# One pair of tiles in a streamed decode kernel: the last 8 KB of each row in loads of 112, 8 and 8 rows

## The chip, the cores and the metric

The kernel runs on one core of a Trainium2 chip. The metric is device time of one execution, in microseconds, median of several runs. The profile is one execution taken by the hardware profiler; its span goes from the first to the last instruction of the program.

## The reference

A decoder layer for one token of each of four sequences (B = 4, D = 512), with modulation from a conditioning vector, cached attention with grouped heads, and a token-mixing MLP:

```python
mod = (_silu(c) @ w_mod).reshape(c.shape[0], 6, 1, -1)
sa, ca, ga, sb, cb, gb = (mod[:, 0], ..., mod[:, 5])
h = _layernorm(x) * (1 + ca) + sa
x = x + ga * attention(h, k_cache, v_cache, wq, wo)
h = _layernorm(x) * (1 + cb) + sb
x = x + gb * mixer(h, w1, b1, w2, b2)
```

Attention has 32 query heads of 128 in groups of four on 8 key/value heads, and 4096 cached positions: q = h @ wq, softmax(q k^T / sqrt(128)) v, then @ wo. The mixer is a layer norm, an outer product with w1 (1792 wide), a gelu and a product with w2. All is float32. The caches are 4 x 8 x 4096 x 128 floats each, 67 MB for the keys and 67 MB for the values; with wq, wo and w_mod 157 MB are read.

## The kernel before

There are NS = 32 tiles, one for each sequence and key/value head. Tile i needs a key tile (128 rows of head dimension x 4096 positions, 16 KB a row) and a value tile (128 rows, each with 32 positions x 128, 16 KB a row). The host lays them out so that `kv[i]` holds the key tile of i + 2 beside the value tile of i: 128 rows of 32 KB, 4 MB, loaded by one transfer in `load_pair` (L176) into a buffer `kv` of shape [128, 2, 4096]. The buffers come from a ring of three (`slots`), shared with wq and parts of w_mod, so a load is issued on the sync engine's queue (SP) when all readers of the load three places before are done.

For each tile the kernel runs, in this order of names: `scores` (L231, 8 matmuls of the key tile against the queries into `s`), `row_max`, `turn_max`, `col_max`, `spread_max`, `copy_max`, `expo` (softmax over 1024 columns x 4 groups of rows, exponentials on the scalar engine), `turn` (a transpose on the vector engine), `sums` and `scale` (the denominators), `values` (L291, 8 matmuls of the value tile against the weights into `pv`; k = 0 to 3 read the first half of each value row, k = 4 to 7 the second half), `copy_v`, `pick`, `copy_o`, `project` (wo) and `add_up`. The mixer of a finished sequence runs in pieces between the tiles of the next.

The instructions of each engine stand in the order in which the program writes them; nothing is reordered. A loop over i = 0 to 23 issues the load of pair i + 1, works on the scores of tile i + 2, and on the values of tile i. Pair 16, issued in the pass i = 15, brings the key tile of 18, read by `scores(18)` in the pass i = 16, and the value tile of 16, read by `values(16, 0..3)` and `values(16, 4..7)` later in the same pass.

The last tiles follow an order written out by hand (a plan of steps). There the key and value tiles come in separate transfers: `load_key` (L197) for keys 30 and 31, `load_v` (L204) for values 28 to 31, the last one cut into five pieces, and `load_wm5` (L192) for the last part of w_mod. The output is written by L575 and L578.

Of the kernel before, what the change touches and what calls it, by code (L numbers as in the profile page):

```python
# [14 lines left out]
B, D, HQ, HKV, SK, DH, F = 4, 512, 32, 8, 4096, 128, 1792  # L15
# [7 lines left out]

WIDE = {NS - 5: 24, NS - 4: 32}
NARROW = NS - 3


@with_exitstack
def adaln_decode(ctx: ExitStack, tc: tile.TileContext, small, x, wmod, wq, kk, kv, vv, wo, out):
    nc = tc.nc  # L30
# [22 lines left out]
    for k in range(0, 4, 2):  # L53
        t = ring.tile([P, 2, HQ * DH], F32, name=f"wq{k}", tag="kv")
# [72 lines left out]
    for k in range(4):  # L127
        n = slice(k * P, (k + 1) * P)
# [20 lines left out]
    rows = cst.tile([B, B, 8], F32, name="rows")  # L149
# [9 lines left out]
    def slots():  # L159
        return ring.tile([P, 2, SK], F32, name="kv", tag="kv")  # L160

    def key(t, i):
        KT[i] = t

    def value(t, i):
        VT[i] = t.rearrange("p (j d) -> p j d", d=DH)
# [6 lines left out]

    def load_pair(i):
        t = slots()
        nc.sync.dma_start(t, kv[i])  # L176
        key(t[:, 0], i + 2)
        value(t[:, 1], i)

# [428 lines left out]

    load_first()
    load_pair(0)  # L610
    load_wo(0)
    for i in range(2):
# [4 lines left out]
    mix = None  # L617
    for i in range(NS - HKV):
        load_pair(i + 1)
        if i in (1, 3, 5):  # L620
            load_wo(i + 1)
# [62 lines left out]
    for step in PLAN.split():  # L684
        op, k = step.rstrip("0123456789."), step.lstrip("abcdefghijklmnopqrstuvwxyzABCDEFGHIJKLMNOPQRSTUVWXYZ")
        i, q = (int(n) for n in (k + ".0").split(".")[:2]) if k else (0, 0)
# [6 lines left out]
        elif op == "v":  # L693
            if i < NS - 2:
                (values if i < NARROW else values_narrow)(i, range(4 * q, 4 * q + 4))
                continue
# [92 lines left out]
```

## Time and profile before

| what | value |
|---|---|
| median of 3 runs | 386.49 us (386.43 to 388.0) |
| span of the profiled execution | 384.7 us (its own time outside the span isn't recorded) |
| TensorE matmul busy (PE) | 298.7 us, 78% |
| vector engine busy (DVE) | 198.2 us, 52% |
| scalar engine busy (ACT) | 112.2 us, 29% |
| bytes moved | 157.69 MB, 410 GB/s over the span |
| mean granted TensorE clock | 0.883 |

How to read it: the page has the busy time of each engine, the span in 40 slices, the transfer queues, the chain of work that ended last (followed back from the last instruction to what released each step), the costliest groups of instructions with the idle time before them, and the transfers with their issue. The trace behind it answers for one stretch of time, one tile or one engine. PE is the matmul engine, PEld its weight loads, SP the sync engine, which here only issues transfers. The transfers of the core run on 16 DMA engines; a share of 1.00 is all of them busy.

### The profile page before, as it was taken

To read this page: it belongs to the slowest core of one execution; us is meant where nothing else is said; L and a number is where in the kernel's file an instruction comes from. 1 tells how busy PE (TensorE), PEld (TensorE's weight loads), DVE (VectorE), ACT (ScalarE), POOL (GpSimd) and SP (SyncE) were. 2 spreads that over 40 slices of the span, in tenths; PEclk is the share of its full clock that TensorE was granted. 3 is DMA by queue.
4 is the path that set the end of the run, shared out by engine and by line. 5 is a ranking of instruction groups with operands and counts; after the bars stand their busy time and mean duration, and the time that the engine had idled before them with its cause. 6 is when DMAs were issued, how large, how long until landed. Compare 5 with 4: busy or idle time off the path is not lost.

```text
span 384.7 us, 5604 instructions
## 1 busy us (share of the span) xinstructions
PE 298.7 (78%) x2380; PEld 117.2 (30%) x2380; DVE 198.2 (52%) x407; ACT 112.2 (29%) x144; POOL 7.7 (2%) x33
## 2 busy tenths in 40 slices
PE   0856777866966949979877878788888887999984
PEld 0112122311323313334322222342222343333653
DVE  1130251620451424664866545557665567778757
ACT  1001111121110110212567311124575105657276
POOL 1100000000000000000000000000000000000000
PEclk9989555985695685998999998999999999999999
DMA  8999999999999999999999999999999999999930
GB/s 331 433 433 436 411 453 433 409 432 436 423 441 433 434 436 436 434 436 431 429 425 433 428 433 434 429 433 431 429 434 436 434 436 432 424 417 423 418 122 3
DMA packets 7409, 157.69 MB, mean 410 GB/s; under 512 B 964, under 2 KB 1236, under 8 KB 1496
## 3 DMA queue, kind: packets, MB, share of 16 engines
q1 hardware_dynamic: 7376, 157.33, 95.4%
q8 instruction: 18, 0.29, 0.3%
q14 instruction: 7, 0.06, 0.0%
q10 hardware_dynamic: 8, 0.00, 0.0%
HBM read 157.32 MB, written 0.01 MB: 409 GB/s over the span
## 4 chain that ended last, share of the span: by engine, by line
DMA 60%; PE 29%; DVE 7%; ACT 2%; issue 1%; POOL 0%; SPq 0%; POOLq 0%; DVEq 0%
DMA kv<-in_kv 58%; PE s L231 8%; PE pv L291 7%; PE s L122 2%; PE qs L138 2%; DVE m L236 2%; DVE p L267 2%; DMA sm<-in_small 2%; PE pa L343 2%; PE pt L328 2%; ACT uu L562 1%; PE pb L251 1%; PE pve L303 1%; PE pm L240 1%; PE pgx L348 1%
## 5 line engine op out<-in xcount | busy, mean ns | idle before, releaser
L231 PE MATMUL s<-kv,QT 128*32 128x512 f32 x512 | 75.2, 714 | 38.9 <-DMA kv<-in_kv 37.0
L236 DVE TENSOR_REDUCE m<-s 128x1 f32<-128x1024 f32 x32 | 39.2, 1224 | 96.0 <-PE s L231 95.9
L261 ACT ACTIVATE p<-s,nm 128x1024 f32<-128x1024 f32 x32 | 35.7, 1115 | 180.6 <-DVE nm L256 180.5
L291 PE MATMUL pv<-kv,p 128*32 128x512 f32 x464 | 69.8, 670 | 0.7 <-DMA kv<-in_kv 0.7
L231 PEld LDWEIGHTS s<-kv,QT 128*32 128x32 f32 x512 | 15.8, 123 | 84.0 <-DMA kv<-in_kv 52.5
L328 PEld LDWEIGHTS pt<-g,po 128*128 128x128 f32 x236 | 31.1, 205 | 27.2 <-issue 19.9
L343 PE MATMUL pa<-wo,oT 128*32 128x512 f32 x240 | 34.6, 648 | 4.6 <-DVE oT L335 4.4
L328 PE MATMUL pt<-g,po 128*128 128x4 f32 (+2 forms) x236 | 33.9, 267 | 1.5 <-DVE po L314 1.0
L267 DVE STREAM_TRANSPOSE p<-p 128x1024 f32<-128x1024 f32 x25 | 30.9, 1234 | 0.0
L314 DVE COPY po<-pv 128x512 f32<-128x512 f32 x29 | 20.0, 688 | 16.8 <-PE pv L291 16.7
L245 DVE TENSOR_REDUCE mx<-pm 1x128 f32<-1x512 f32 x32 | 21.3, 669 | 1.1 <-PE pm L240 1.1
L442 DVE TENSOR_SCALAR u<-hb,wr,sm 128x512 f32<-128x512 f32 x40 | 19.9, 541 | 1.9 <-POOL wr L437 1.0
L506 ACT ACTIVATE u<-u 128x1024 f32<-128x1024 f32 x20 | 20.4, 1051 | 1.5 <-DVE u L442 1.4
L361 DVE TENSOR_TENSOR acc<-acc,pa 128x512 f32<-128x512 f32 x26 | 17.8, 686 | 4.3 <-PE pa L343 4.2
L261 ACT ACT_TABLE_LOAD x11 | 14.1, 1283 | 20.3 <-DVE nm L256 20.2
L251 PEld LDWEIGHTS pb<-neg,mx 1*128 1x128 f32 x64 | 10.4, 202 | 28.2 <-DVE mx L245 26.5
L122 PE MATMUL s<-wm,sT 128*4 128x512 f32 x16 | 9.1, 732 | 10.6 <-DVE sT L108 10.6
L506 ACT ACT_TABLE_LOAD x13 | 16.7, 1283 | 0.2
L291 PEld LDWEIGHTS pv<-kv,p 128*32 128x32 f32 x464 | 13.4, 146 | 7.2 <-issue 3.1
L240 PE MATMUL pm<-ident,m 128*1 128x128 f32 x32 | 9.3, 289 | 7.4 <-DVE m L236 3.5
L251 PE MATMUL pb<-neg,mx 1*128 1x1 f32 x64 | 13.1, 271 | 2.1 <-DVE mx L245 2.1
L453 PE MATMUL py<-u,sm 128*32 128x512 f32 x80 | 14.4, 616 | 0.0
(158 smaller groups left out, 214.7 us busy)
## 6 DMA issues: line engine op xcount, KB each, us to landing
kv<-in_kv SPq DMA_DIRECT2D x28, 4096.0 KB, 21.9
wq<-in_wq SPq DMA_DIRECT2D x2, 4096.0 KB, 16.3
wo<-in_wo SPq DMA_DIRECT2D x4, 2048.0 KB
kv<-in_kv SPq DMA_DIRECT2D x4, 2048.0 KB, 20.3
wm<-in_wmod SPq DMA_DIRECT2D x2, 2048.0 KB, 14.8
kv<-in_kk SPq DMA_DIRECT2D x1, 4096.0 KB
kv<-in_vv SPq DMA_DIRECT2D x3, 1024.0 KB
wm<-in_wmod SPq DMA_DIRECT2D x1, 1024.0 KB
```

Source lines behind the costliest of these rows:

```text
L231: mm(s[32 * c:32 * c + 32, n * 512:(n + 1) * 512], QT[:, b, h, :], KT[i][:, (n * 4 + c) * 512:(n * 4 + c + 1) * 512], start=True, stop=True)
L236: dv.tensor_reduce(M[i], S[i], axis=AX.X, op=OP.max)
L245: dv.tensor_reduce(mx, M[i].rearrange("o (c r) -> o r c", c=4).unsqueeze(1).to_broadcast([1, 4, 32, 4]), axis=AX.X, op=OP.max)
L251: mm(pb, M[i].rearrange("o c r -> o (c r)"), neg1, start=True, stop=True)
L261: nc.scalar.activation(p, S[i], AF.Exp, bias=M.pop(i), accum_out=l)
L267: dv.transpose(PL[i][0], PL[i][0])
L291: mm(PV[i][32 * q:32 * q + 32, :], pT[:, 128 * k:128 * k + 128:4], VT[i][:, 4 * k:4 * k + 4, :].rearrange("p j d -> p (j d)"), start=(k < ...
L314: dv.tensor_copy(PV[i], pv)
L328: mm(pt, po[:, c * DH:(c + 1) * DH], sel.unsqueeze(1).to_broadcast([P, m, REP]), start=(c == 0), stop=(c == n - 1))
L343: mm(pa[32 * g:32 * g + 32, :], oT[:, g:g + 1].to_broadcast([P, 32]), wo_t[h][:, g, :], start=True, stop=True)
L442: dv.tensor_scalar(u[:, e, :], hb, wr[:, j:j + 1], b1[:, j:j + 1], op0=OP.mult, op1=OP.add)
L506: nc.scalar.activation(u, u, AF.Gelu_apprx_tanh)
```

## The change

The load of pair 16 is cut. The first 24 KB of each row (the key tile and the first half of the value tile) come in one transfer of 128 rows. The last 8 KB of each row (the second half of the value tile) come in three: rows 0 to 111, rows 112 to 119, rows 120 to 127. The same bytes go to the same places; all other loads stay as they are.

```diff
 WIDE = {NS - 5: 24, NS - 4: 32}
 NARROW = NS - 3
+UNEVEN = 16
...
     def load_pair(i):
         t = slots()
-        nc.sync.dma_start(t, kv[i])
+        if i == UNEVEN:
+            main = SK + SK // 2
+            rows, src = t.rearrange("p s n -> p (s n)"), kv[i].rearrange("p s n -> p (s n)")
+            nc.sync.dma_start(rows[:, :main], src[:, :main])
+            for lo, hi in ((0, 112), (112, 120), (120, 128)):
+                nc.sync.dma_start(rows[lo:hi, main:], src[lo:hi, main:])
+        else:
+            nc.sync.dma_start(t, kv[i])
         key(t[:, 0], i + 2)
         value(t[:, 1], i)
```

## The prediction

> **What bounds the kernel now.** I read the slices of the page first, then the chain that ended last, the stretches of time around the changed load and at the end of the stream, and then the matmul timeline at the places where the chain passes from transfers to matmuls.
>
> The page's slices (tenths of each fortieth of the span, then what the transfers moved) and its table of queues:
>
> ```profile
> DMA  8999999999999999999999999999999999999930
> GB/s 331 433 433 436 411 453 433 409 432 436 423 441 433 434 436 436 434 436 431 429 425 433 428 433 434 429 433 431 429 434 436 434 436 432 424 417 423 418 122 3
> ...
> q1 hardware_dynamic: 7376, 157.33, 95.4%
> q8 instruction: 18, 0.29, 0.3%
> ...
> DMA 60%; PE 29%; DVE 7%; ACT 2%; issue 1%; POOL 0%; SPq 0%; POOLq 0%; DVEq 0%
> ```
>
> The transfer engines are busy in every slice up to the thirty-eighth, at about 430 GB/s, and 60% of the chain is waiting for them. So up to about 370 us the kernel is a stream of bytes, and 430/16 = 26.9 GB/s is what one of the 16 engines moves: an 8 KB row piece is 8192/26.9 = 0.30 us of one engine. 157.33 MB in 7376 packets is 21 KB a packet, so rows travel whole or nearly so, not chopped into small pieces. The 18 instruction packets held an engine for 0.003 x 16 x 384.7 / 18, about 1.0 us each (an estimate from a rounded share); they fall on single engines, so they can push engines apart.
>
> The chain in order of time (start, length, what), at the changed load and at the last load that it waits for:
>
> ```profile
> 208.57 21.85 DMA kv<-in_kv
> 230.47 3.32 PE s L231 x16
> ...
> 239.28 21.41 DMA kv<-in_kv
> ...
> 268.00 21.70 DMA kv<-in_kv
> ...
> 327.22 15.81 DMA kv<-in_kv
> 343.04 0.14 issue
> 343.17 1.92 PE s L231 x16
> ```
>
> The load issued at 208.57 is the one that changes (pair 16, the seventeenth issue of L176). It lands at 208.57 + 21.85 = 230.42. From 239.28 + 21.41 = 260.69 to 268.00 + 21.70 = 289.70 lie three loads, so one takes 9.67 us, and the changed one was issued 21.85 - 9.67 = 12.2 us before the engines could turn to it. The last transfer on the chain is the half load with key 30, landing at 343.03. Behind it the chain is matmuls, vector and scalar work almost without a gap, 384.7 - 343.2 = 41.5 us. So a delay of the slowest transfer engine anywhere earlier in the stream that is still there at 343 is a delay of the end.
>
> Stretches of time (busy us of PE, PEld, DVE, ACT, POOL with counts, clock, DMA share, GB/s):
>
> ```profile
> 200.00:210.00 10.00, 7.70 (x61) 2.83 (x61) 6.75 (x14) 7.34 (x9) 0.00 (x0) 1.00 0.99 429
> ...
> 300.00:320.00 20.00, 17.20 (x147) 8.38 (x149) 12.00 (x27) 3.69 (x5) 1.31 (x3) 1.00 1.00 430
> ...
> 343.00:360.00 17.00, 15.91 (x172) 7.88 (x176) 13.90 (x33) 10.59 (x13) 0.00 (x0) 1.00 1.01 428
> ...
> 366.50:367.00 0.50, 0.50 (x28) 0.47 (x22) 0.38 (x2) 0.50 (x1) 0.00 (x0) 1.00 0.81 305
> ...
> 368.00:369.00 1.00, 1.00 (x19) 0.88 (x22) 0.40 (x3) 0.86 (x2) 0.00 (x0) 1.00 0.56 238
> 369.00:370.00 1.00, 0.87 (x40) 0.60 (x28) 0.16 (x1) 0.06 (x1) 0.00 (x0) 1.00 0.22 82
> ```
>
> The last rows show the engines running out at different times. A share of 0.56 is nine of sixteen still at work in 368 to 369, and seven had finished by then; the first began to run out in 366.5 to 367. Every big load gives each engine the same bytes, so nine engines are some 2 to 3 us behind seven. The engines are not in step, and the slowest sets each landing. The changed load hands unequal bytes to them, and that is what has to be priced.
>
> **The change, part by part.**
>
> *Issue.* One load of 128 rows x 32 KB becomes 128 x 24 KB, 112 x 8 KB, 8 x 8 KB and 8 x 8 KB: three more issues on SP. The SP rows of the transfer lines and of SP's own waits:
>
> ```profile
> L176 SPq DMA_DIRECT2D kv<-in_kv x28: 327/328/328, 30.1 to 316.1; - x28
> ...
> 327.22 0.81 SPq L197 DMA_DIRECT2D kv<-in_kv  x2
> ...
> SPq L176 <- PE pv L291: 186.4, 23, 12.3
> ```
>
> Two issues back to back took 0.81 us, so three more cost about 3 x 0.40 = 1.2 us of SP. It is hidden by the 12.2 us of queue above, and SP waits 186.4/23 = 8.1 us on average before such a load for its buffer, so the next issue isn't late either. Without that cover it would be 1.2 us. Cost: 0.
>
> *More packets.* Each engine handles eight row pieces more, and up to three completions. The stretch 343 to 360, whose loads have rows of 16 KB and less, ran at 428 GB/s, that of 300 to 320 with whole 32 KB rows at 430: 0.5%, on one load 0.05 us. Not below zero, since nothing gets shorter. Cost: +0.05 us on every engine.
>
> *Unequal bytes.* Of the last 8 KB, 112 rows are seven for each of 16 engines; the other 16 rows go in two loads that can occupy at most eight engines each if a row goes whole, as the packet size says. No row of the page shows which. Bounds: if the two loads use different eights, every engine again has eight rows, 0; if one engine took all sixteen rows, it would carry 7 + 16 instead of 8, 15 x 0.30 = +4.5 us. In between, the same eight engines twice: nine rows for those (+0.30 us) and seven for the others (-0.30 us). I take this, because equal loads issued alike have no reason to go to different engines and the full loads show spreading as far as rows allow. With the packets: +0.35 us on eight engines, -0.25 us on eight.
>
> The Trainium skill, "DMA: Bandwidth & Descriptors", section "Why a DMA increments its semaphore by 16 and not by 1", says the number of engines is the largest up to 16 that divides the row count, on this kind of queue the lowest-numbered ones. By it the sum would be the same +0.35 and -0.25 us, and the bounds 0 and 4.5 would fall away.
>
> *Which engines are late.* Nine are late and only eight can be without the extra row, so at least one late engine gets it. Whether that is the very latest decides: the late nine lie within about 1 us of each other (share 0.56 falls to 0.22 in 369 to 370). So the landing at 343.03 moves by between -0.25 and +0.35 us. I take +0.3.
>
> *Earlier and later landings inside the load.* The key half and the first half of the values now come with the 24 KB part, so S of tile 18 may start 1.05 MB / 430 = 2.4 us earlier, while the second half of values(16) waits for three loads. The matmul timeline there:
>
> ```profile
> 226.91 1.09 PE L291 MATMUL pv<-kv,p 128*32 128x512 f32 x8
> 230.47 3.26 PE L231 MATMUL s<-kv,QT 128*32 128x512 f32 x16 [2.46 <-DMA kv<-in_kv]
> ...
> 238.17 1.04 PE L291 MATMUL pv<-kv,p 128*32 128x512 f32 x8
> 241.56 1.92 PE L231 MATMUL s<-kv,QT 128*32 128x512 f32 x16 [2.35 <-DMA kv<-in_kv]
> ```
>
> PE's idle 2.46 us before 230.47 goes, and comes back as a longer wait before 241.56, because the next load isn't earlier. Even with tile 18's work moved up by 2.4 us, the second half of the values starts at 235.8, 5.4 us behind the old landing at 230.42, so the small loads may be up to 5.4 us late before any matmul notices. Added waits on PE stand in that idle time, with scores(19) queued behind them. If the cover were gone, each us there would be one on PE only until the next wait for a transfer. Gain and cost: 0.
>
> *At the end.* The wait that decides, from the same timeline:
>
> ```profile
> 342.19 0.38 PE L275 MATMUL pl<-g,l 128*128 128x4 f32 x2
> 343.17 1.92 PE L231 MATMUL s<-kv,QT 128*32 128x512 f32 x16 [0.60 <-DMA kv<-in_kv]
> ```
>
> PE stood idle 0.60 us for key 30. An earlier landing gains at most 0.60; a later one costs in full, since nothing before it can be done instead in a fixed order.
>
> **Sum**: 0 + 0 + 0.3 us. The span goes from 384.7 to 385.0; the median of the runs shown, 386.49, lies 1.8 us above the span (what surrounds it and other executions), which the change doesn't touch. Forecast 386.49 + 0.3 = 386.8 us.
>
> **Rivals.**
>
> *Slower: neighbouring rows get in each other's way on the write side.* In a full load each engine has rows of its own for the whole load; in an 8-row load eight engines write eight neighbouring rows at the same time. If rows in a group of four share one way into the memory with an engine's rate, four pieces take 4 x 0.30 = 1.2 us instead of 0.30, so the two loads add 2 x 0.9 = 1.8 us, with the 0.35 together 2.1 us: 388.6. It decides at 343 only above the lead an engine has; the late ones have none. If the eight rows of one load go one by one, it is 2 x 7 x 0.30 + 0.35 = 4.5 us: 391.0. The 112-row load, with seven rows an engine out of step with the groups, would add to it, and a next load's rows on the same ways too. For it: every stretch at 430 GB/s is of loads of 128 rows, so the trace holds no sign that other shapes run as fast. Against it: it needs engines that arrive together, and they are 2 to 3 us apart at the end against pieces of 0.30 us.
>
> The Trainium skill, "SBUF — State Buffer", section "Door 1: The DMA port swizzle", has this rule: four neighbouring partitions share a port at one engine's rate. By it 388.6 would be the floor of this rival and the uneven 112 rows would push it higher. No row here shows it.
>
> *Relief.* The very latest engines are all among those with seven rows: -0.25 us, 386.2. For it: the extra row goes to eight, the lag to nine, and both may be fixed halves. Against: one of the nine must have the extra row.
>
> *The change doesn't do what it says.* The 8-row loads are spread evenly after all: +0.05 us, 386.5.
>
> *Clearly faster* would take 1.9 us. The late engines lose at most 0.25 us and PE's wait holds 0.60; I see no place for it.
>
> **How the numbers follow.** About 0.5%, 1.9 us, is what a measurement of this kernel can tell from no change. Forecast (+0.3, up to 1 us where engines collide a little) 0.33; relief 0.19; no effect 0.10; crowded rows 0.35, nearly all above 1.9 us since the floor is 2.1, 0.33 of it; clearly faster 0.03. Same: 0.33 + 0.19 + 0.10 + 0.02 = 0.64. The first three lie in 386.1 to 387.5; that is the likeliest case's own range, with relief. To leave out no more than two in ten the range has to reach into the crowded rows: 386.0 to 390.5.
>
> **What would show it.** In the profile after: four issues in place of one under the kv lines, 27 whole pairs. S of tile 18 about 2.4 us earlier and a wait of some 4.8 us before tile 19. GB/s in the slice around 220 to 230 us: unchanged if engines keep their rate; for the crowded rows a dip, 2 us of eight engines being some 430 x 2 x 0.5 = 430 KB missing from the 10 us, 43 GB/s of one window. The landing of key 30 at 343.3 by the forecast, 342.8 by relief, 345 or later by crowding, with the chain behind it as long as before. The stretches at the end: nine engines late as before, or more of them if the extra row pushes an early one back. It would be wrong if the landing at 343 moves without the end, or if SP's issue of the next load comes late.

## The result, and the profile after

The changed kernel takes 390.14 us (median of 6 runs, 389.69 to 391.67), the kernel before beside it 386.51 us. The ratio is 1.0096, 95% interval 1.0072 to 1.0119: slower by 3.6 us. (Ratios in this document compare the means of the runs, so a few high runs move them more than the medians; one run of the 4 KB cut below, 396.68 us, counts as slow and is left out of its ratio.) The profiled execution has a span of 387.9 us against 384.7, so 3.2 us of it can be followed in the trace.

The page's slices after (tenths of each fortieth of the span, then what the transfers moved):

```profile
DMA  8999999999999999999999999999999999999920
GB/s 328 433 433 433 421 443 433 419 442 433 419 444 433 431 433 431 433 433 431 433 431 433 426 319 425 433 436 427 433 431 433 431 433 428 422 424 427 417 118 3
```

One slice, the twenty-fourth (223 to 233 us), moves 319 GB/s instead of about 430. The share of busy transfer engines stays at nine tenths there. So the engines weren't idle; they were slower at the same work. The stretch 220 to 240 us, before and after (last number GB/s, the one before it the share of the 16 engines):

```profile
220.00:240.00 20.00, 15.51 (x122) 5.51 (x117) 10.35 (x21) 2.41 (x4) 0.00 (x0) 0.91 1.00 433
```

```profile
220.00:240.00 20.00, 14.10 (x122) 5.32 (x114) 10.54 (x21) 2.41 (x4) 0.00 (x0) 0.98 1.02 372
```

(433 - 372) x 20 us = 1.2 MB are missing, at 433 GB/s 2.8 us of the whole stream. That is most of the 3.2 us. The chain of waits after, in order of time, shows where it arrives:

```profile
218.17 26.14 DMA kv<-in_kv
244.36 3.64 PE s L239 x16
...
330.07 15.94 DMA kv<-in_kv
...
346.14 1.92 PE s L239 x16
```

The load behind the changed one (pair 17, a plain load) lands at 244.31. Key 30, the last transfer on the chain, lands at 346.01 instead of 343.03: 2.98 us later. Behind it lie 387.9 - 346.1 = 41.8 us, before 41.5. The scores of tile 19, which wait for pair 17, start at 244.36 instead of 241.56, 2.80 us later. So nearly all of the delay arises in one place, is carried through a hundred microseconds of stream, and is paid in full at the end.

The matmul timeline around the changed load (start, length, engine, line, operation, idle time before):

```profile
229.53 1.92 PE L239 MATMUL s<-kv,QT 128*32 128x512 f32 x16 [1.43 <-DMA kv<-in_kv]
...
235.88 1.04 PE L299 MATMUL pv<-kv,p 128*32 128x512 f32 x8
...
244.36 3.64 PE L239 MATMUL s<-kv,QT 128*32 128x512 f32 x16 [7.43 <-DMA kv<-in_kv]
```

The second half of the values (235.88) has no wait before it: the three small loads were never late for a matmul. In the trace the load of 112 rows ends with 16 completion signals and each load of 8 rows with 8, the last at 234.1; that fits 16 engines and 8, as the forecast counted. But scores of tile 18 start only 0.9 us earlier than before (230.47), not 2.4, and the wait before tile 19 is 7.43 us, not 4.8. The stretches at the end of the stream:

```profile
369.00:370.00 1.00, 1.00 (x47) 0.89 (x36) 0.78 (x3) 0.80 (x1) 0.00 (x0) 1.00 0.99 386
370.00:371.00 1.00, 0.98 (x16) 0.58 (x8) 0.29 (x1) 0.99 (x2) 0.00 (x0) 1.00 0.59 249
371.00:372.00 1.00, 1.00 (x18) 0.88 (x21) 0.40 (x3) 0.75 (x2) 0.00 (x0) 1.00 0.54 229
372.00:373.00 1.00, 0.79 (x36) 0.52 (x28) 0.16 (x1) 0.14 (x1) 0.00 (x0) 1.00 0.14 49
```

The pattern is that of before moved by 3 us: some nine engines of sixteen at work in the last but one microsecond (0.54 now, 0.56 before), and the early ones run out 3 us later too. All engines were held up about alike. It isn't a matter of eight that carry more.

### The profile page after: what moved, and what is told of

Same layout as the page of the kernel before. It is cut to its first block, busy times and chain, and to the rows that moved or that the text cites. A ratio compares the mean times of both kernels' runs of the same rounds, so it can differ in the third digit from the quotient of the medians.

```text
span 387.9 us, 5609 instructions
## 1 busy us (share of the span) xinstructions
PE 294.8 (76%) x2380; PEld 117.2 (30%) x2380; DVE 198.5 (51%) x407; ACT 112.2 (29%) x144; POOL 7.7 (2%) x33
## 4 chain that ended last, share of the span: by engine, by line
DMA 59%; PE 29%; DVE 7%; ACT 2%; issue 1%; POOL 0%; SPq 0%; POOLq 0%; ACTq 0%
DMA kv<-in_kv 46%; PE s L239 9%; PE pv L299 7%; DMA wm<-in_wmod 6%; DMA kv<-in_kk 5%; DVE m L244 3%; PE s L123 2%; DMA sm<-in_small 2%; DVE p L275 2%; PE pb L259 1%; ACT uu L570 1%; PE pt L336 1%; PE pa L351 1%; PE pve L311 1%; PE pm L248 1%
## 5 line engine op out<-in xcount | busy, mean ns | idle before, releaser
L336 PEld LDWEIGHTS pt<-g,po 128*128 128x128 f32 x236 | 31.7, 209 | 27.5 <-issue 19.4
## 6 DMA issues: line engine op xcount, KB each, us to landing
kv<-in_kk SPq DMA_DIRECT2D x1, 4096.0 KB, 18.5
```

The lines of the kernel that those rows point to most:

```text
L336: mm(pt, po[:, c * DH:(c + 1) * DH], sel.unsqueeze(1).to_broadcast([P, m, REP]), start=(c == 0), stop=(c == n - 1))
```

## The experiments

Two theories were put against each other. *Unequal bytes*: only the number of rows that each engine carries counts (the forecast's own sum). *Crowding*: engines that write rows which they don't write in a full load get in the way of others (the first rival, in a wider form: any such row, not only neighbouring ones). A third, a price by pieces or issues, was kept beside them. The first four runs change how the last 8 KB are cut.

**One even load for the last 8 KB.**

```diff
-            for lo, hi in ((0, 112), (112, 120), (120, 128)):
+            for lo, hi in ((0, 128),):
```

> The last 8 KB of the rows of pair 16 come as one load of 128 rows, not as 112, 8 and 8; the 24 KB part stays. Crowding (rows written by engines that do not usually write them collide): 386.5 us, within 0.3 of the kernel before, and the stretch 220 to 240 us back at about 430 GB/s, since all loads have 128 rows again. Unequal bytes alone: also 386.5. Price of more pieces and issues: most of the 3.6 us stays, 389 or more.

Measured 386.61 us beside 386.43, ratio 1.0006 (0.9994 to 1.0018). The stretch 220 to 240 us and the scores of tile 18:

```profile
220.00:240.00 20.00, 13.93 (x118) 5.32 (x114) 10.53 (x21) 2.41 (x4) 0.00 (x0) 1.00 1.01 432
...
228.23 1.92 PE L239 MATMUL s<-kv,QT 128*32 128x512 f32 x16
```

The dip is gone, and tile 18 now starts 2.2 us earlier than before, without a wait. Cutting the rows at 24 KB costs nothing measurable. A price by pieces falls: this kernel has as many 8 KB rows as the changed one, 128. It has one issue more than the kernel before, not three; a price by issue falls further down, where two issues more cost 0.51 us together with their bytes (rows four apart).

**112 and 16 rows.**

```diff
-            for lo, hi in ((0, 112), (112, 120), (120, 128)):
+            for lo, hi in ((0, 112), (112, 128)):
```

> The last 8 KB come as 112 and 16 rows, so that each of 16 engines has seven rows and one row, eight as before. Unequal bytes alone: 386.5 us, nothing left. Crowding: the 112 rows are still out of step with the usual places and the 16 rows are neighbours, so most stays: 388.5 to 390, and the stretch 220 to 240 us stays below 400 GB/s.

Measured 389.88 us, ratio 1.0082 (1.0061 to 1.0104), +3.45 us, and 372 GB/s in the stretch, as in the changed kernel. Both loads end with 16 completion signals, which fits seven rows and one for each of 16 engines. Unequal bytes fall as the cause.

**64 and 64 rows.**

```diff
-            for lo, hi in ((0, 112), (112, 120), (120, 128)):
+            for lo, hi in ((0, 64), (64, 128)):
```

> The last 8 KB come as two loads of 64 rows, four rows for each of 16 engines in each, equal bytes. Unequal bytes alone: 386.5 us. Crowding, if 64 neighbouring rows have half of the ways: 0.5 MB at half the rate twice, 2 x 1.2 = 2.4 us more than the 2.4 us that they take now, so 388.9 us, with a dip of about 1 MB in the stretch 220 to 240 us.

Measured 389.97 us, ratio 1.0086 (1.0065 to 1.0108), +3.54 us:

```profile
220.00:240.00 20.00, 14.21 (x122) 5.38 (x122) 10.53 (x21) 2.41 (x4) 0.00 (x0) 1.00 1.01 366
```

Same loss, with no 8-row load at all. Crowding had 388.9; it is 1.1 us more than that. The expectation counted only the two loads themselves. The plain load behind them suffered too: its 32 KB rows took up to 2318 ns, where 1213 ns is usual (see "Row by row" below). That engines out of step are still at one half while others are at the next load fits this, but no run shows it apart.

**The same cut on 4 KB.**

```diff
-            main = SK + SK // 2
+            main = SK + SK * 3 // 4
```

> As the changed kernel, but the last 4 KB of each row instead of 8 KB are cut into 112, 8 and 8 rows. Crowding goes by bytes: half of the 3.6 us, about 388.3 us. Unequal bytes alone: half of 0.35 us, 386.7. A price by piece or by issue: the same 390 us as with 8 KB.

Inconclusive. The median is 389.51 us, ratio 1.0087 (1.0058 to 1.0116), but the ten runs lie between 388.34 and 396.68; five of them between 388.3 and 388.9, +1.9 to +2.5 us, near the half that crowding has. The others lie between 390.1 and 396.7. The last section comes back to it.

The next runs leave pair 16 whole and add loads behind it, so that the cost of each shape stands alone. They read a part of wo again into the place where it already lies. The first two ("neighbours" and "four apart" below):

```diff
         nc.sync.dma_start(t, kv[i])
+        if i == 16:
+            for lo, hi in ((112, 120), (120, 128)):
+                nc.sync.dma_start(wo_p[1][lo:hi, 1], wo[1][lo:hi, 1])
```

> Pair 16 is loaded whole as before; behind it two loads of 8 neighbouring rows (112 to 119, 120 to 127) of 8 KB are added, which read a part of wo again into the place where it already lies; the result is unchanged, 128 KB more are moved. Unequal bytes alone: eight engines carry two rows more, 0.6 us, so 386.9 to 387.2 us. Crowding: the eight neighbouring rows take four times as long, 1.2 us a load, so 388 to 389 us.

```diff
         nc.sync.dma_start(t, kv[i])
+        if i == 16:
+            for e in range(2):
+                nc.sync.dma_start(wo_p[1][0:32:4, e], wo[1][0:32:4, e])
```

> As the run with 8 neighbouring rows added, but the rows of each added load are 0, 4, ... 28, four apart, so that no two of one load stand in a group of four. Unequal bytes alone: the same 386.9 to 387.2 us as with neighbours. Crowding by groups of four: nothing on top of the bytes, so also 386.9 to 387.2 us, 1 to 2 us less than with neighbours.

Neighbours: 388.42 us beside 386.46, ratio 1.0053 (1.0036 to 1.0070), +1.96. Four apart: 386.97, ratio 1.0019 (1.0008 to 1.0030), +0.51. The same bytes in the same number of rows differ by 1.45 us. The stretch 220 to 240 us, neighbours first:

```profile
220.00:240.00 20.00, 15.38 (x100) 5.95 (x104) 7.91 (x14) 1.21 (x2) 0.00 (x0) 0.77 1.01 406
```

```profile
220.00:240.00 20.00, 16.49 (x105) 5.94 (x103) 8.84 (x15) 1.20 (x2) 0.00 (x0) 0.78 1.01 435
```

(435 - 406) x 20 = 0.58 MB, 1.3 us at 435 GB/s, close to the difference in time. Each added load ends with eight completion signals, and the packets of the run with rows four apart, strung together without gaps, put one row of each load on the same eight engines. So +0.51 us for two rows more on eight engines is the byte term of the forecast (0.60) nearly at its size.

**112 or 128 rows added.**

```diff
         nc.sync.dma_start(t, kv[i])
+        if i == 16:
+            nc.sync.dma_start(wo_p[1][0:112, 1], wo[1][0:112, 1])
```

> Pair 16 is loaded whole; behind it one load of 112 rows of 8 KB is added (wo again into its own place). Bytes alone: seven rows an engine, 2.1 us, 388.6 us. Crowding by rows out of step: on top 1 to 2 us, 389.6 to 390.6 us.

```diff
         nc.sync.dma_start(t, kv[i])
+        if i == 16:
+            nc.sync.dma_start(wo_p[1][:, 1], wo[1][:, 1])
```

> Pair 16 is loaded whole; behind it one load of 128 rows of 8 KB is added (wo again into its own place). Both theories: the bytes, eight rows an engine, 2.4 us, 388.9 us. Measured beside the 112 rows: crowding has this one at the same time or faster although it moves more, bytes alone has it 0.3 us slower.

112 rows: 391.73 us, ratio 1.0135 (1.0120 to 1.0150), +5.27. 128 rows: 388.99, ratio 1.0067 (1.0052 to 1.0082), +2.53, the 2.4 us of its bytes. Sixteen rows fewer cost 2.7 us more. The stretch, 112 rows first:

```profile
220.00:240.00 20.00, 14.35 (x114) 5.29 (x110) 8.79 (x16) 1.21 (x2) 0.00 (x0) 0.91 1.01 367
```

```profile
220.00:240.00 20.00, 13.92 (x118) 5.32 (x114) 10.53 (x21) 2.41 (x4) 0.00 (x0) 1.00 0.99 427
```

Seven rows are 7 x 0.304 = 2.13 us, so the 112-row load alone costs 5.27 - 2.13 = 3.1 us above its bytes, more than the upper 2 us of the expectation and nearly the whole of the changed kernel's loss.

**Which side is crowded.** A second copy of wo in memory has the rows needed moved, so that reading and writing can be varied apart. Shown is only the load that is added behind pair 16; the second copy, wx, is made on the host.

```diff
+        if i == 16:
+            for e, lo in enumerate((112, 120)):
+                nc.sync.dma_start(wo_p[1][lo:lo + 8, 1], wx[32 * e:32 * e + 32:4, 1])
```

> The two added loads write neighbouring rows (112 to 119, 120 to 127) but read rows that lie four apart in memory (a second copy of wo with these rows moved; the result is unchanged). If the crowding is where the rows are written: as with neighbours on both sides, 388.4 us. If it is where they are read: as with rows apart on both sides, 387.0 us.

```diff
+        if i == 16:
+            for e, lo in enumerate((112, 120)):
+                nc.sync.dma_start(wo_p[1][0:32:4, e], wx[lo:lo + 8, 1])
```

> The two added loads write rows 0, 4, ... 28 but read neighbouring rows of the second copy. If the crowding is on the writing side: 387.0 us, as with rows apart on both sides. If on the reading side: 388.4 us.

Writing neighbours, reading apart: median 388.42 us, ratio 1.0064 (1.0037 to 1.0091), seven of ten runs within 388.26 to 388.44, the others up to 393.08. Writing apart, reading neighbours: median 387.36, ratio 1.0040 (1.0012 to 1.0068), six of ten within 386.77 to 387.44, the others up to 391.74. The stretch, in the same order:

```profile
220.00:240.00 20.00, 14.75 (x118) 5.50 (x114) 8.91 (x17) 1.37 (x3) 0.00 (x0) 0.91 1.01 405
```

```profile
220.00:240.00 20.00, 14.04 (x122) 5.32 (x114) 10.54 (x21) 2.41 (x4) 0.00 (x0) 1.00 1.00 432
```

The loss follows the rows that are written (405 as with neighbours on both sides, 432 as with rows apart on both), though the intervals of the two times overlap. The transfer rates decide here, and they are those of one execution each.

**Rows apart, but others' rows.**

```diff
+        if i == 16:
+            for e in range(2):
+                nc.sync.dma_start(wo_p[1][64:96:4, e], wo[1][64:96:4, e])
```

> The two added loads write and read rows 64, 68, ... 92, four apart as in the run with rows 0 to 28. If only pieces of one load in the same group of four disturb each other: 387.0 us again. If a row also disturbs the engine that writes that group in the full loads, and rows 64 to 92 belong to eight other engines than the eight of the added loads: each row shares its way with one full load's row, 0.3 us a row on both, so 387.5 to 388.2 us.

Median 388.63 us, ratio 1.0084 (1.0048 to 1.0120), six of ten runs within 388.33 to 388.63, the others up to 393.31:

```profile
220.00:240.00 20.00, 15.51 (x100) 5.87 (x96) 8.20 (x15) 1.20 (x2) 0.00 (x0) 0.76 1.00 405
```

Rows four apart cost as much as neighbours if they are rows 64 to 92 instead of 0 to 28. So the loss doesn't need rows that are near each other within one load. The median is above the expectation's upper 388.2. The 8-row loads that cost time all write rows above 63, and no run added neighbouring rows below, so whether nearness adds something isn't shown.

The Trainium skill, "DMA: Bandwidth & Descriptors", section "The descriptor swizzle", gives for a transfer of 128 rows which engine writes which rows: rows 0, 4, ... 28 belong to the first eight engines in order, rows 64, 68, ... 92 to the other eight. By that page, if the added loads run on the first eight engines and these take the rows in order, the run with rows 0, 4, ... 28 has each engine at its own rows and this one at another's, and the traces agree: 435 against 405 GB/s. That the added loads run on the first eight engines is the same page's rule (section "Why a DMA increments its semaphore by 16 and not by 1"). The traces show eight engines for each load but don't name them.

**Row by row.** The trace also lists each packet, here one row of one load, with its own time. An 8 KB row took 309 ns, every one of them, in the even cut, with 128 rows added and in both runs that write rows 0, 4, ... 28; a 32 KB row of a plain load takes 1213 ns. Where time was lost, rows took longer. What they took beyond these times, summed over the rows that start between 225 and 236 us and divided by 16 engines, comes close to the loss:

| run | 8 KB rows, beyond their usual time | rows of the loads before and behind | sum / 16 |
|---|---|---|---|
| the changed kernel | 27.8 us | 19.8 us | 3.0 us |
| 112 rows added | 26.9 us | 22.7 us | 3.1 us |
| neighbours added | 2.0 us | 19.4 us | 1.3 us |
| rows 64 to 92 added | 1.4 us | 18.5 us | 1.2 us |

The sixteen rows added as neighbours took 6.9 us in all, the longest 0.67. An owner that stood still for the whole of each of them would have lost 6.9 us; the plain rows lost 19.4. At 232.0 us in that run all sixteen rows on their way are plain ones, and each takes 1329 to 1926 ns. So the disturbance spreads from a few foreign rows to all engines and outlasts most of them. How it spreads isn't shown.

## Why the prediction was right or wrong

The time fell inside the range, in the part that had been added for the crowded rows; the forecast itself, +0.3 us, was not what happened. The rival that the range was widened for had 388.6 as its centre and expected the loss in other loads, so that the range held is in part luck. Step by step:

- *Issue, cover zero*: right. The SP rows after show three issues of 295 to 423 ns, and no load behind them was late for it.
- *More packets, +0.05 us*: right. In the even cut a row takes 912 + 309 ns in two pieces and 1213 ns in one, 8 ns more, on eight rows 0.06 us. The run is at +0.18 us with an interval that holds zero.
- *Unequal bytes, +0.35 and -0.25 us*: **the step that failed**. The count of rows was right as far as the trace shows it (16 completion signals for the 112 rows, 8 for each of the small loads). The price was not. The sum priced a row at the engine's full rate (8192/26.9) whatever load it stands in. That rate was read in loads of 128 rows alone. In the 112-row load, which the sum took as seven rows at full rate, it doesn't hold: added alone, its rows took 556 ns in the median, not 304, and the loads around it lost as well, 3.1 us above the bytes in all. The count of rows per engine was no cause: 112 and 16 rows, equal for all, lose 3.45 us.
- *Nine late engines, one of which must have the extra row*: a right reading of the stretches that decided nothing, since all engines were delayed by 3 us.
- *Scores of tile 18 earlier by 2.4 us*: right for the even cut (2.2 us, at 228.23), not for the changed kernel (0.9 us). The 24 KB part itself was late: ten of its 128 rows, all among the last, took 1134 to 1655 ns instead of 912, while early engines were already at the 112 rows.
- *Cover for the small loads until 235.8*: right, no wait before 235.88, and the last of them had landed at 234.1.
- *The end pays for key 30 in full*: right, 2.98 us at the landing, 3.2 us of the span.
- *The rival of crowded rows*: right in place and sign, wrong in its centre. It put the weight on the two 8-row loads (1.8 us) and left the 112-row load as something that "would add to it". Measured, 8-row loads of neighbours cost 1.45 us more than the same loads with rows four apart, and the 112-row load 3.1 us above its bytes; together, inside pair 16, 3.6 us. No row of the added neighbours took the 1.2 us of the rival's price, the longest 0.67; most of their loss lies in the plain loads. The costs don't add, and 112 with 16 rows is within 0.3 us of 112, 8 and 8. The argument held against it, that engines 2 to 3 us apart seldom meet, didn't hold: 116 of the 128 rows of 8 KB in the changed kernel took longer than 309 ns. That a foreign row meets an owner busy with its own load, just because they are out of step, fits this; it is argued, not shown.
- *The Trainium skill's rule on ports* ("SBUF — State Buffer", section "Door 1: The DMA port swizzle"), cited there with 388.6 us as a floor: the traces agree with it in that the loss goes with the rows written (405 against 432 GB/s when only these differ), and the measured 390.1 lies above that floor. They don't bear out the price: the floor stood on four rows that take four times 0.30 us, and none did.

What isn't settled: how a few foreign rows slow all engines. And of the 3.1 us of the 112 rows, 1.7 lie in its own rows and 1.4 in the plain loads, but whether its own rows met each other or plain ones no run tells apart.

## What to carry to other kernels

In this kernel the stream kept its 430 GB/s with loads of 128 rows and with added rows 0, 4, ... 28, which fits the reading that each engine then writes rows of its own. Loads of 112, of 64 and of 8 other rows lost time themselves and in the full loads around them, and as the kernel is bound by transfers the loss arrived at the end undiminished. Cut long rows by columns, over all 128 rows (+0.18 us here, with an interval that holds zero), not by rows (+3.5 us). And a rate read in one shape of load is a price for that shape only: when a change brings another shape, the bound must come from the rival, not from the rate.

## What the runs showed that was not expected

The disturbance can last. In the profiled execution of the 4 KB cut (392.32 us) plain loads of 128 rows stay slow for some 30 us behind the cut, after the cut loads were done:

```profile
230.00:240.00 10.00, 9.11 (x43) 3.30 (x43) 3.88 (x6) 0.00 (x0) 0.00 (x0) 0.51 1.03 374
240.00:250.00 10.00, 7.14 (x65) 2.76 (x61) 5.40 (x12) 1.21 (x2) 0.00 (x0) 1.00 0.97 375
250.00:260.00 10.00, 6.94 (x40) 2.79 (x36) 3.42 (x9) 1.21 (x2) 0.55 (x1) 0.68 1.04 400
260.00:270.00 10.00, 10.00 (x45) 5.09 (x48) 3.29 (x8) 2.56 (x4) 0.76 (x2) 0.50 0.96 385
...
300.00:320.00 20.00, 17.11 (x136) 6.83 (x135) 9.32 (x18) 3.01 (x5) 0.00 (x0) 0.91 1.00 430
```

374 to 400 GB/s where only plain loads run, then 430 again. The last 4 KB row ends at 232.1 us; from there to about 265 us the 32 KB rows of all engines take about 1359 ns instead of 1213. Why the engines stay in it and what ends it was not tried.

A second effect sits on top of some runs. In the profiled execution of the run with rows 64 to 92 (393.31 us, the highest of its ten) the granted TensorE clock (third number from the end) fell late in the stream:

```profile
302.00:312.00 10.00, 8.28 (x69) 3.79 (x65) 5.39 (x10) 1.50 (x3) 0.00 (x0) 1.00 1.01 436
312.00:322.00 10.00, 9.21 (x50) 2.71 (x42) 4.67 (x13) 0.00 (x0) 0.55 (x1) 0.52 1.03 441
322.00:332.00 10.00, 9.55 (x53) 5.29 (x52) 5.19 (x11) 3.03 (x3) 0.76 (x2) 0.63 0.98 424
```

Transfers go on at 424 to 441 GB/s, but the matmuls fall behind: the sixteen score matmuls of a tile take 3.57 us at 318.13, against 1.85 at 346.07 with the clock back at 1.00. That execution's chain has its last wait for a transfer at 311.1 us, and none for key 30. So with the clock down that close to the end the matmuls set the end here. Whether the other high runs have the same cause isn't shown.
